# Five bursts of attention scores in place of six, in two of a fused kernel's eight batches

## The chip, the core and the metric

The kernel runs on one core of one Trainium2 chip. The metric is device time in microseconds (us), the whole program from start to end. The core has five engines with a queue each: TensorE (PE in the profile; its weight loads are listed apart as PEld), VectorE (DVE), ScalarE (ACT), GpSimd (POOL) and SyncE (SP). Here POOL and SP do little but issue DMAs. Each engine works its queue in order, and semaphores tell one engine that another is done.

## What is computed

The reference is sigmoid attention followed by a gated feed-forward layer, cut here to what matters:

```python
scores = scale * np.matmul(q, k.transpose(0, 1, 3, 2)) - np.log(S)   # 8 batches, 12 heads, S = 448, head size 64
attn = 1.0 / (1.0 + np.exp(-scores))
x = np.matmul(attn, v)                   # then heads beside each other: 3584 tokens x 768
gate = np.maximum(x @ w_gate, 0.0)       # 768 x 1536
out = (gate * (x @ w_val)) @ w_out       # 1536 x 768
```

## The kernel before, in words

**Units.** The attention of a batch is cut into 21 *units* `(g, c)`: 3 groups `g` of four heads, and 7 chunks `c` of 64 keys. `qk_unit` (line 299 and on) runs a unit: two PSUM banks are taken, `qk` (L239) writes scores for two pairs of heads into them with four matmuls that each use a quarter (64x64) of the PE array and run at the same time, and two sigmoids on ACT (L187), one for each bank, put the result into a tile `PT` in SBUF (11 such tiles, used in turn). When the 7 units of a group are there, `pv` (L257) multiplies them with `v`: 28 quarter-array matmuls into two banks, which DVE copies to `xT` (L184).

**Works.** Between the units PE does the feed-forward layer of batches that are through with attention, in full-array (128x128) matmuls, L389. It comes in *works* taken from a queue by `next_work`. Two kinds matter. `gv_pair`, the gate and value pair (`"w"`, six for each group of two batches), makes two slices of 128 features of gate and value for two batches by a Strassen-like scheme of seven products of six matmuls each, in this order: `u`, `g2`, `u` again, `g1`, `u`, `g2`, `u`. ACT or DVE copies the first `u` (L644), ACT copies `g2` and the second `u` (L624), DVE adds (L628) and makes `hT` (L638). `down_pair` (`"y"`) makes the output from `hT`, also in seven products. Each work prepares on DVE the weight sums of the next (`prepare`).

**Order.** The order on all engines is that in which the Python code issues (`manual_schedule`). The loop over batches `b` = 1 to 7 (L934 and on) cuts the 21 units at `cuts` into bursts. Step `m` issues one burst and then one work, so that ACT can do the burst's sigmoids while PE works. `pv_at` says where in a burst a `pv` is slipped in: at index 2 of burst 0 for the last group of the batch before, of burst 2 for group 0 and of burst 4 for group 1. In batch 4 there are six bursts of 4, 3, 4, 3, 4, 3 units, and the six works are the gate and value pairs of batches 2 and 3. In batch 6 the works are one `down_pair`, with burst 1 in its middle (`inner`), and four gate and value pairs of batches 4 and 5, each behind a burst. So the even bursts have four units and a `pv`, and the odd ones three units.

**Banks.** PSUM has 8 banks. `bank()` hands them out in the order of a queue and puts each at its end; `later` reorders it. A unit or a `pv` takes two neighbours, called a *pair of banks* below. A gate and value pair takes three pairs of banks, for `u`, `g2` and `g1`, and leaves the queue so: the pair of banks it did not use, then `g1`, `g2`, `u`. A burst begins at the head of that queue.

**Transposes and loads.** `dma_transposes(b, g)` makes `qkT` for group `g`: two DVE copies into a tile `rel` (L222) and a transposing DMA from SP (L226). `load` and `load_v` (L111 to L117, POOL) fetch the next batch; `k` and `q` have one buffer, so their loads wait for the last group's `rel` copies. These steps are jobs of a work: they are issued in its middle (`beside`), behind its third product.

The lines that set all this are:

```python
cuts, pv_at = (0, 4, 7, 11, 14, 18, 21), {0: (-1, 2), 2: (0, 2), 4: (1, 2)}
...
for m in range(count):
    jobs, ahead = [], []
    burst(bursts[m])
    if m == (2 if b == 4 else 0) and b > 3:
        jobs.append(lambda: dma_transposes(b, 2))
    ...
    elif 0 <= m - count + 2 and b in (4, 6):
        jobs.append(lambda: dma_transposes(b + 1, m - count + 2))
    ...
    elif m == (2 if b == 4 else 0) and b + 1 < B:   # load(b + 1, ...), load_v(b + 1)
```

Of the kernel before, what the change touches and what calls it, by code (L numbers as in the profile page):

```python
# [18 lines left out]
def kernel(  # L19
# [170 lines left out]
    def qkT_of(b, g):  # L190
        if (b, g) not in qkT_tiles:
            qkT_tiles[(b, g)] = qkTp.tile([P, TW, P], FP16, tag="qkT", name="qkT")
        return qkT_tiles[(b, g)]
# [24 lines left out]
    def dma_transposes(b, g):  # L218
        k16, q16, _ = in_tiles[b]
        rel = relp.tile([P, TW, P], FP16, tag="rel", name="rel")  # L220
        for ti, t16 in enumerate((k16, q16)):
            nc.vector.tensor_copy(  # L222
                rel[:, ti * NCH : (ti + 1) * NCH, :].rearrange("p c (h d) -> p h c d", h=2),
                t16[:, 2 * g : 2 * g + 2, :].rearrange("p h (c d) -> p h c d", c=NCH),
            )
        nc.sync.dma_start_transpose(  # L226
            qkT_of(b, g)[:], rel[:].rearrange("p c x -> p (c x)")
        )
# [70 lines left out]
    def qk_unit(b, g, c):  # L299
        ps = [bank("qk_ps") for _ in range(2)]  # L300
        qk(qkT_tiles[(b, g)], c, 0, NCH, lambda hh: ps[hh][:, 0:S])
        PT = PTp.tile([P, 2, S], FP16, tag="PT", name="PT")
        for hh in range(2):
            sigmoid(PT[:, hh, 0:S], ps[hh][:, 0:S])
        PT_tiles[(b, g, c)] = PT

    def pv_group(b, g):
        pv(b, g, 0, S, [PT_tiles.pop((b, g, c))[:, :, 0:S] for c in range(NCH)])


    def gv(b, q0, qn, f, act_relu):
        gv_out(b, q0, qn, f, act_relu, [gv_product(b, q0, qn, f, i) for i in range(2)])
# [247 lines left out]
    def early_sum_steps(j, f):  # L560
        views = []
        for i in range(3 * j, 3 * j + 3):
            t = early.tile([P, 2, 512], FP16, tag=f"PT{i}", name="S")
            flat = t[:].rearrange("p a y -> p (a y)")[:, 0 : HD * 2 * P]
            views.append(flat.rearrange("p (x y) -> p x y", y=2 * P))
        yield lambda: gate_sums(f, f + 2)
        yield from unit_sum_steps(("s", f), f, views)
# [292 lines left out]
    def pv_finish(b):  # L860
        pv_group(b, NG - 1)
# [7 lines left out]
    def both(b, g):  # L869
        pe_transposes(b, g, 0)  # L870
        pe_transposes(b, g, 1)
# [32 lines left out]
    def prepare():  # L904
        for step in prepare_steps():
            step()

    def next_work(jobs=(), alone=False, amid=None, ahead=()):
        kind, g, i = work.popleft()

        due = pending[:]
        del pending[:]

        def beside():
            for job in due + list(jobs):
                job()

        for job in ahead:
            job()
        if kind == "y":  # L920
            down_pair(g, i, beside, prepare, not work, scaled_act if alone else scaled, amid)
        elif amid:
            raise ValueError(kind)
        elif kind == "w":
            by = (nc.vector.tensor_copy, nc.scalar.copy)
            gv_pair(g, i, lambda: (prepare(), beside()), (by[alone], by[alone or bool(ahead)]))
        elif kind == "s":
            gv_split(g, i, lambda: (prepare(), beside()))
        else:
            gv(g, 0, S, i, True)  # L930
            beside()
            prepare()

    for b in range(1, B):  # L934
        if b == 1:
            cuts, pv_at = (0, 3, 6, 9, 13, 17, 21), {3: (0, 2), 5: (1, 2)}
        else:
            cuts, pv_at = (0, 4, 7, 11, 14, 18, 21), {0: (-1, 2), 2: (0, 2), 4: (1, 2)}
        bursts = list(range(len(cuts) - 1))
        inner = {}  # L940
        if b > 2:
            inner = {2: 3, 3: 5} if b == B - 1 else {0: 1, 1: 3, 2: 5} if b % 2 else {} if b == 4 else {0: 1}
            for n in inner.values():
                bursts.remove(n)
        count = len(bursts)
        hooks = {}
        if b == 1:
            mix = (4, 3, 3, 3, 3, 4)
            hooks = {
                1: [(3, lambda: both(1, 1))],  # L950
                3: [(3, lambda: both(1, 2))],
                4: [(2, lambda: dma_transposes(2, 0)), (0, lambda: dma_transposes(2, 1))],
                5: [(4, late_loads)],
            }
            steps = itertools.chain.from_iterable(early_sum_steps(j, 2 * j) for j in range(4))
            given = ((0, 0, 1, 1, 1), (0, 1, 1, 1), (0, 1, 1, 1), (0, 1, 1, 0), (2, 0, 0, 0), (0, 1, 1, 1, 0))
        else:
            mix = (0,) * count

        def burst(n):  # L960
            for i, (g, c) in enumerate(order[cuts[n] : cuts[n + 1]]):
                if n in pv_at and i == pv_at[n][1]:
                    if n == 0:
                        pv_finish(b - 1)
                        if b == 2:
                            push_group(0)
                        elif b == 6:
                            push_group(2)
                    else:
                        pv_group(b, pv_at[n][0])  # L970
                qk_unit(b, g, c)

        for m in range(count):
            jobs, ahead = [], []
            burst(bursts[m])
            if m == (2 if b == 4 else 0) and b > 3:
                jobs.append(lambda: dma_transposes(b, 2))
            if b == 2 and m == 3:
                jobs += [lambda: dma_transposes(3, 0), lambda: dma_transposes(3, 1)]
            elif b == 3 and m == count - 1:  # L980
                jobs.append(lambda: dma_transposes(4, 1))
                push_group(1)
            elif b == 5 and m == count - 1:
                jobs += [lambda: dma_transposes(6, 0), lambda: dma_transposes(6, 1)]
            elif 0 <= m - count + 2 and b in (4, 6):
                jobs.append(lambda: dma_transposes(b + 1, m - count + 2))
            if b == 1:
                if m == 0:
                    load(2, 0, 1, "kq")
                    load(2, 1, 2, "kq")  # L990
                    load(2, 2, 3, "kq")
            elif m == (2 if b == 4 else 0) and b + 1 < B:
                for g0, g1 in ((0, 1), (1, NG)) if b == 3 else ((0, NG),) if b > 3 else ():
                    jobs.append(lambda g0=g0, g1=g1: load(b + 1, g0, g1, "kq"))
                jobs.append(lambda: load_v(b + 1))
            if b == 2 and m == 0:
                ahead.append(lambda: split_sums(1))
            elif b == 2 and m == 4:
                open_late()
                first_sums = token_sum_steps(0, 0)  # L1000
                ahead += [*first_sums[:2], lambda: weight_sums(0)]
            elif b == 2 and m == 5:
                ahead += [lambda: weight_sums(1), lambda: dma_transposes(3, 2)]
                jobs += first_sums[2:]
            elif b == 3 and m == 0:
                jobs.append(lambda: (weight_sums(2), weight_sums(3)))
            elif b == 3:
                jobs.append(lambda: gate_sums(6 + 2 * m, 8 + 2 * m))
                if m == 1:
                    jobs.append(lambda: keep_odd(0))  # L1010
            if b % 2 and b > 2:
                if m == count - 1:
                    jobs.append(lambda: (batch_sums_t1(b // 2), batch_sums(b // 2, (0, 1))))
            elif b == 4 and m == 0:
                first, *others = batch_sum_steps(1, (1, HD))
                ahead.append(first)
                jobs = others + jobs
            elif b > 3 and m == 0:
                jobs.append(lambda: batch_sums(b // 2 - 1, (1, HD)))
            if mix[m]:  # L1020
                for job in jobs:
                    job()
                ffn_mix(mix[m], hooks.get(m, ()), steps, given[m])
            else:
                next_work(
                    jobs, ahead=ahead,
                    amid=(lambda: burst(inner[m])) if m in inner else None,
                )
            if b == 3 and m == count - 2:
                dma_transposes(4, 0)  # L1030
    pv_finish(B - 1)
    push_group(B // 2 - 1)
    next_work([lambda: batch_sums(B // 2 - 1, (1, HD))])
# [32 lines left out]
```

## Time and profile before

| what | value |
|---|---|
| time, median of 3 runs | 388.31 us (388.07 to 388.63) |
| the profiled execution | 388.3 us |
| its span, first to last instruction | 386.5 us |
| granted TensorE clock, mean | 0.999 of full speed |
| busy share PE, PEld, DVE, ACT, POOL | 99%, 58%, 79%, 59%, 13% |
| batch 4 in the span | 125.6 to 182.6 us |
| batch 6 in the span | 212.8 to 260.7 us |

The span is 1.8 us less than the profiled execution's own time; what lies around it is start and end. In the timeline each row is a run of like instructions: start, length, engine, line, what is written and read, how many, and in brackets how long the engine sat idle before it and what ended that. Rows of PE overlap, because matmuls are pipelined: the distance between the starts of two rows is the time that PE gives to the first, and the length of a row is a little longer.

### The profile page before, as it was taken

What the parts mean: (1) busy time and instruction counts of PE and PEld (TensorE: products, weight loads), DVE (VectorE), ACT (ScalarE), POOL (GpSimd) and SP (SyncE); (2) the same over time, 40 slices, a digit from 0 to 9 for tenths busy, and PEclk for the clock granted to TensorE, in tenths of its full rate; (3) what the DMA queues carried; (4) which work ended last, traced back from release to release, by engine and by line L of the source; (5) the groups of instructions that cost most, each with busy time, mean ns of one, the idle gap of its engine ahead of it and who ended that gap; (6) DMA issues with size and microseconds to landing.
All of it is one profiled execution on the core that took longest, in us unless ns stands there. A gap on an engine that the chain in (4) does not pass through costs nothing.

```text
span 386.5 us, 8978 instructions
## 1 busy us (share of the span) xinstructions
PE 381.1 (99%) x3570; PEld 223.2 (58%) x3570; DVE 304.9 (79%) x611; ACT 227.3 (59%) x480; POOL 49.8 (13%) x73
## 2 busy tenths in 40 slices
PE   8999999999999999999999999999999999999996
PEld 6678776885555545455555554545455555555654
DVE  3455667769868999999868789999978788999653
ACT  5967887567777645455777764545477344333322
POOL 8643306100400003000300300000000000000000
PEclk9999999999999999999999999999999999999999
DMA  9999999999979302952499893222013220000235
GB/s 171 199 199 204 204 193 161 208 208 135 179 168 178 81 2 37 182 95 47 43 229 220 171 233 56 44 54 50 0 28 76 72 75 0 2 0 0 73 92 165
DMA packets 67563, 43.81 MB, mean 113 GB/s; under 512 B 35648, under 2 KB 64192, under 8 KB 67520
## 3 DMA queue, kind: packets, MB, share of 16 engines
q0 software_dynamic: 28960, 23.24, 39.2%
q1 hardware_dynamic: 37792, 19.34, 24.5%
q10 hardware_dynamic: 768, 0.66, 0.6%
q8 instruction: 28, 0.46, 0.5%
q14 instruction: 15, 0.12, 0.1%
HBM read 47.19 MB, written 11.01 MB: 151 GB/s over the span
## 4 chain that ended last, share of the span: by engine, by line
PE 96%; ACT 2%; DMA 1%; DVE 0%; issue 0%
PE u L389 34%; PE g L389 16%; PE y L389 12%; PE qk_ps L239 10%; PE pv_ps L257 8%; PE g_ps L322 5%; PE v_ps L322 5%; PE u L718 2%; PE g L718 2%; ACT PT L187 2%; DMA qkT<-rel 1%; PE warm_ps L175 1%; PE trt L204 1%; DVE ysb L544 0%; DVE zeros L130 0%
## 5 line engine op out<-in xcount | busy, mean ns | idle before, releaser
L187 ACT ACTIVATE PT<-qk_ps 128x448 f16<-128x448 f32 (+3 forms) x318 | 150.9, 584 | 79.2 <-PE qk_ps L239 79.1
L389 PEld LDWEIGHTS <-S 128*128 128x128 f16 x576 | 56.3, 98 | 45.9
L628 DVE TENSOR_TENSOR gsb<-g,gsb 128x448 f32<-128x448 f32 x72 | 42.7, 623 | 7.9 <-PE g L389 7.5
L239 PE MATMUL qk_ps<-qkT 64*64 64x448 f16 (+2 forms) x756 | 47.5, 337 | 0.7 <-DMA qkT<-rel 0.3
L389 PEld LDWEIGHTS <-hT 128*128 128x128 f16 x318 | 29.5, 98 | 24.0 <-issue 6.1
L257 PE MATMUL pv_ps<-PT,v 64*64 64x448 f16 (+2 forms) x756 | 36.6, 329 | 0.0
L468 DVE SCALAR_TENSOR_TENSOR ysb<-y,ysb 128x384 f32<-128x384 f32 x33 | 18.3, 555 | 20.7 <-PE y L389 14.1
L184 DVE TENSOR_SCALAR xT<-pv_ps 128x448 f16<-128x448 f32 (+2 forms) x53 | 27.8, 566 | 8.0 <-PE pv_ps L257 6.9
L389 PEld LDWEIGHTS <-wg 128*128 128x128 f16 x216 | 20.2, 98 | 21.8 <-issue 4.3
L389 PEld LDWEIGHTS <-wv 128*128 128x128 f16 x216 | 21.1, 98 | 19.7
L450 ACT ACTIVATE ysb<-u 128x384 f32<-128x384 f32 x28 | 13.8, 491 | 30.9 <-PE u L389 26.8
L389 PE MATMUL u<-wo,hT 128*128 128x384 f16 x156 | 29.8, 327 | 0.0
L239 PEld LDWEIGHTS <-qkT 64*64 64x64 f16 x756 | 17.6, 106 | 21.0 <-issue 14.1
L111 POOL DMA_DIRECT2D k<-in_k_dram x14 | 10.8, 775 | 141.0 <-DVE rel L222 135.9
L257 PEld LDWEIGHTS <-v 64*64 64x64 f16 x756 | 21.4, 107 | 11.1 <-issue 0.5
L389 PE MATMUL u<-xT,wg 128*128 128x448 f16 x108 | 23.5, 354 | 0.0
L389 PE MATMUL u<-xT,wv 128*128 128x448 f16 x108 | 23.4, 352 | 0.0
L389 PE MATMUL g<-X,S 128*128 128x448 f16 x108 | 23.4, 352 | 0.0
L389 PE MATMUL u<-X,S 128*128 128x448 f16 x108 | 23.4, 352 | 0.0
L389 PE MATMUL g<-xT,S 128*128 128x448 f16 x108 | 23.4, 352 | 0.0
L389 PE MATMUL g<-xT,wg 128*128 128x448 f16 x108 | 23.4, 352 | 0.0
L389 PE MATMUL u<-X,wv 128*128 128x448 f16 x108 | 23.4, 352 | 0.0
(98 smaller groups left out, 563.9 us busy)
## 6 DMA issues: line engine op xcount, KB each, us to landing
out_dram<-ysb SPq DMA_DIRECT2D x53, 192.0 KB, 3.1
v<-in_v_dram POOLq DMA_DIRECT2D x8, 336.0 KB, 15.3
v<-in_v_dram POOLq DMA_DIRECT2D x16, 168.0 KB, 15.1
k<-in_k_dram POOLq DMA_DIRECT2D x4, 672.0 KB, 11.6
q<-in_q_dram POOLq DMA_DIRECT2D x4, 672.0 KB, 14.8
wo<-in_moe_w_out_dram POOLq DMA_DIRECT2D x2, 1152.0 KB, 19.2
k<-in_k_dram POOLq DMA_DIRECT2D x9, 224.0 KB, 11.8
q<-in_q_dram POOLq DMA_DIRECT2D x7, 224.0 KB, 12.3
```

What stands on the lines that cost most here:

```text
L111: nc.gpsimd.dma_start(t16[:, xs, cs], rows_of(src, b)[:, xs, cs])
L175: nc.tensor.matmul(ps[:, 0:n], zeros[:, 0:P], zeros[:, 0:n], start=True, stop=True)
L184: nc.vector.tensor_scalar(out=xT, in0=src, scalar1=XSCALE, scalar2=None, op0=AOP.mult)
L187: nc.scalar.activation(PT_ap, ps_ap, AF.Sigmoid, bias=sig_bias, scale=qk_scale)
L239: nc.tensor.matmul(out_of(hh)[o : o + 64, :], qkT[rows, c, cols], qkT[rows, NCH + c0 : NCH + c1, cols], start=True, stop=True, tile_positi ...
L257: nc.tensor.matmul(ps[hh][64 * r : 64 * r + 64, 0:qn], v16[rows, 2 * g + hh, c * D : (c + 1) * D], pieces[c][rows, hh, :], start=(c == 0), ...
L322: nc.tensor.matmul(ps[:, 0:qn], (wg, wv)[i][:, dc, f * P : (f + 1) * P], xT_tiles[b][:, dc, q0 : q0 + qn], start=(dc == 0), stop=(dc == ND ...
L389: nc.tensor.matmul(ps[:, 0:n], A[:, k_, :], W[:, k_, :], start=(first and k_ == 0), stop=(k_ == kn - 1), skip_group_check=True,)
L450: nc.scalar.activation(o, ps[:, 0:HM], AF.Copy, scale=OUT_SCALE)
L468: nc.vector.scalar_tensor_tensor(out=o, in0=ps[:, 0:HM], scalar=OUT_SCALE, in1=o, op0=AOP.mult, op1=AOP.add)
L628: nc.vector.tensor_tensor(out=gs[u][i][:], in0=ps[u][:, 0:S], in1=gs[u][i][:], op=AOP.add)
L718: nc.tensor.matmul(ps[j // 2][:, j % 2 * SQ : (j % 2 + 1) * SQ], sets[j][i][:, k_, :], W[:, k_, :], start=(first and j % 2 == 0 and k_ == ...
```

## The change

In batches 4 and 6 the cuts become 0, 5, 8, 13, 16, 21: five bursts of 5, 3, 5, 3, 5 units. The places of `pv` stay at index 2 of bursts 0, 2 and 4. `count` falls by one in both batches, from 6 to 5 and from 5 to 4. The last gate and value pair of each batch (slices 10 and 11 of batches 2 and 3; slices 6 and 7 of batches 4 and 5) now follows the pair before it directly; it is called with `alone=True`, which puts both copies of its first product on ACT rather than DVE, and it has no jobs. In batch 4 the transposes of the last group move from step 2 to step 1. The transposes for the next batch stay in the last two steps of the loop, which are now one step earlier.

```diff
-            cuts, pv_at = (0, 4, 7, 11, 14, 18, 21), {0: (-1, 2), 2: (0, 2), 4: (1, 2)}
+            cuts = (0, 5, 8, 13, 16, 21) if b in (4, 6) else (0, 4, 7, 11, 14, 18, 21)
+            pv_at = {0: (-1, 2), 2: (0, 2), 4: (1, 2)}
...
-            if m == (2 if b == 4 else 0) and b > 3:
+            if m == (1 if b == 4 else 0) and b > 3:
                 jobs.append(lambda: dma_transposes(b, 2))
...
             if b == 3 and m == count - 2:
                 dma_transposes(4, 0)
+        if b in (4, 6):
+            next_work((), True)
     pv_finish(B - 1)
```

## The prediction

> **What bounds the kernel now.** First the page's busy shares and the waits of PE, then the timeline of one stretch of batch 6, engine by engine.
>
> ```profile
> PE 381.1 (99%) x3570; PEld 223.2 (58%) x3570; DVE 304.9 (79%) x611; ACT 227.3 (59%) x480; POOL 49.8 (13%) x73
> ...
> PE 96%; ACT 2%; DMA 1%; DVE 0%; issue 0%
> ```
>
> ```profile
> PE warm_ps L175 <- DVE zeros L130: 1.2, 1, 1.2
> PE qk_ps L239 <- DMA qkT<-rel: 0.3, 1, 0.3
> PE qk_ps L239 <- ACT PT L187: 0.3, 1, 0.3
> ```
>
> The chain that ended last is 96% PE, and PE's waits add up to 1.8 us. So a microsecond that PE gains or loses in batches 4 and 6 is one gained or lost at the end. Now PE, ACT and DVE around a burst of three units, the pair behind it, and a burst of four with a `pv`:
>
> ```profile
> 231.76 1.30 PE L389 MATMUL u<-X,wv 128*128 128x448 f16 x6
> 232.98 0.76 PE L239 MATMUL qk_ps<-qkT 64*64 64x448 f16 x12
> 233.68 1.31 PE L389 MATMUL u<-xT,wg 128*128 128x448 f16 x6
> 234.82 1.30 PE L389 MATMUL g<-X,S 128*128 128x448 f16 x6
> ...
> 241.73 0.57 PE L239 MATMUL qk_ps<-qkT 64*64 64x448 f16 x8
> 242.13 1.49 PE L257 MATMUL pv_ps<-PT,v 64*64 64x448 f16 x28
> 243.45 0.55 PE L239 MATMUL qk_ps<-qkT 64*64 64x448 f16 x8
> ```
>
> ```profile
> 242.21 3.60 ACT L187 ACTIVATE PT<-qk_ps 128x448 f16<-128x448 f32 x8 [4.28 <-PE qk_ps L239]
> 245.85 1.10 ACT L624 COPY gsb<-g 128x448 f32<-128x448 f32 x2
> ```
>
> ```profile
> 242.37 1.15 DVE L638 SCALAR_TENSOR_TENSOR hT<-gsb 128x448 f16<-128x448 f32 x2
> 243.66 1.16 DVE L184 TENSOR_SCALAR xT<-pv_ps 128x448 f16<-128x448 f32 x2
> 244.73 1.17 DVE L644 COPY gsb<-u 128x448 f32<-128x448 f32 x2
> ```
>
> Look at the pace of ACT. PE puts out a unit in 0.19 us; ACT needs two sigmoids for it. Eight took 3.60 us, one alone 0.56, so they start (3.60 - 0.60) / 7 = 0.43 us apart, the last at 0.60: 0.85 us for each unit. Within a burst PE outruns ACT by far, and only the four pairs of banks let it.
>
> **What it saves: two bursts' entry and exit.** A full-array product takes 1.135 us (six matmuls, 233.68 to 234.82), 0.189 for each. The next pair's first product starts at 243.94, so from pair to pair (233.68 to 243.94) it is 10.26 us: 42 matmuls x 0.189 = 7.95, four units and seven rounds of `pv` 11 x 0.189 = 2.08, and 0.23 left. For the burst of three (224.94 to 233.68): 8.74 - 7.95 - 0.57 = 0.22. The row starts say where this lies: PE leaves the last product 0.09 late for the burst (231.76 + 1.135 + 0.09 = 232.98) and the burst 0.10 late for the product. A burst costs about 0.23 whatever its size. Two fewer: **-0.46 us**. The units and products themselves keep their number: in the order of the instructions PE has 7142 rows before and after.
>
> Here a rule of the Trainium skill bears on it: TensorEngine Tiling (Array Packing), section Key Properties, says that a change of the tiling mode drains TensorE. The entry and exit rows agree, with 0.09 and 0.10 us. If each were a full drain of about 175 ns, as TensorE: Matmul & The Clock Gate, section Single matmul latency, has it, two bursts less would be an estimated -0.70 and the sum 389.3; the rows decide.
>
> **What it adds: the fifth unit waits for the second's sigmoids.** Follow the bank queue, as the front describes it: L (left over), A (old `g1`), C (old `g2`), B (old `u`). In a burst with `pv` at index 2 the takers are u0 on L, u1 on A, `pv` on C, u2 on B, u3 on L, and now u4 on A. u4 may not write until both sigmoids of u1 are done. From the rows, with S = 241.73 the burst's start: u2 at S + 1.72, u3 + 1.91, u4 would be at S + 2.10. ACT begins at S + 0.48; u1's second sigmoid is its fourth: start S + 0.48 + 3 x 0.43 = S + 1.77, length 0.56, end S + 2.33 (this row alone, by the timeline: 243.50 + 0.56 = 244.06). From ACT's end to PE's start there are 0.05 to 0.06: the early first-slot sigmoids end at 7.94 + 1.93 = 9.87, and the matmul that waits for them starts at 9.93:
>
> ```profile
> 9.93 0.30 PE L239 MATMUL qk_ps<-qkT 64*64 64x256 f16 x4 [0.28 <-ACT PT L187]
> ```
>
> So u4's second matmul starts at S + 2.38, **0.28 late**. PE's queue is in order: the burst's exit and the pair behind it stand behind that matmul, and nothing hides it. ACT cannot be earlier, as it was idle 4.28 us before the burst and starts when the first unit's matmuls are done. u3 on L is free: u0's sigmoids end at S + 1.46.
>
> There are six such bursts: 0, 2, 4 in both batches. In all, u4's bank is last read by u1's sigmoids. Where a copy to `ysb` precedes the sigmoids (bursts 0 of both and 2 of batch 6) ACT still starts at S + 0.49 to 0.50. Sum: 6 x 0.28 = **+1.69 us**. Bounds for one wait: 0, if the release came 0.28 earlier than these rows say; 0.4, if as much is added as PE waited for the one late transpose (PEld idle for 0.70 at 212.79, 0.32 ahead of the other bursts behind a `down_pair`). I take 0.28, since all its terms are rows of this very burst.
>
> **What else moves, and its cover** (each taken as 0):
> - The pair behind a five-unit burst takes C, B, L. C is read by DVE's two `xT` copies: second ends S + 3.09; the second half of the first product, which needs it, starts at S + 2.10 + 0.28 + 0.29 + 0.57 = S + 3.24. Spare 0.1. B's sigmoids (u2) end near S + 3.2, used at S + 3.8; L's (u3) S + 4.1, used at S + 6.1.
> - ACT has two more sigmoids before the `g2` copies: 0.85 later in ACT's queue, 0.47 later on PE, so 0.4 of delay. The second `u` copies follow and must be done when the fifth product begins, at pair + 4.54. They end 0.1 to 0.4 before it.
> - The lone sixth pair takes L, A, C, all read long before; its first copies on ACT start at 0.73 and 1.3 into the pair, and the third product needs them at 2.27. DVE loses 1.17 of work there.
> - Batch 4's `rel` copies for group 2 and, released by them, SP's transpose and POOL's five loads come one pair earlier (about 9.3 us; POOL only sat waiting, 49.88 us, for these copies). The transpose took 11.9 us beside those loads (150.98 to 162.89); issued at 141.6, it lands at 153.5, and unit 14 needs it at 156. Spare 2.5, against 0.7 before. k and q landed 12.2 and 15.4 after the first load's issue: 157.0, used at 160.4. In batch 6 the copies for batch 7 come about 9 us earlier, at 239; their q lands at 234.4. Uncovered, each microsecond late would cost one, once.
> - `PT`: unit 18's tile is unit 7's, read in the first round of the `pv` just before it, S + 0.6; its sigmoid comes at S + 2.2.
>
> **Sum**, on the profiled execution's 388.3 (span 386.5, 1.8 around it; the median of the runs, 388.31, is the same): 388.3 - 0.46 + 1.69 = **389.5 us**, 0.3% slower. About 0.2% (0.78 us) is what a measurement of this kernel can tell from no change.
>
> **Rivals.**
> 1. *The banks come free in time* (0.12). Only the saving stays: 388.3 - 0.46 = 387.8, not slower. Place: u4's second matmul. It decides if ACT's fourth sigmoid releases its bank at S + 2.05 or before, 0.28 sooner than its row ends. For it: bursts of four never wait for ACT. Against: in a burst of four only u3 takes a pair of banks for the second time, and there it has 0.4 of spare.
> 2. *The backlog reaches the pair too* (0.08). The 0.1 of spare at DVE's `xT` copies or ACT's copies is gone, and each of six pairs loses 0.2 to 0.3 more: 389.5 + 6 x 0.25 = 391.0. For it: DVE has no idle row around bursts, its `hT` rows end only 0.14 before the `xT` rows. Against: with `rel` copies in the pair ahead, DVE is as early at the next burst (before 260.73 it reaches `hT` 0.42 ahead of it, just as before 241.73).
> 3. *A late transpose or load* (0.02): the spares above are used up; 390 to 392.
> 4. *The clock falls* (0.02). PE's granted clock is 9 tenths or more in all 40 slices, and 0.999 in the mean, with a gap of 0.38 us in it. If six new gaps took half the clock for one slice (9.7 us), it would cost 4.8: 394.3. The Trainium skill, TensorE: Matmul & The Clock Gate, section A second HAM failure mode: psum-queue depth-cycling, tells of such a case, where short idles from cycling through banks made the clock oscillate; this trace, with its 0.38 us gap at full clock, doesn't bear it out.
>
> The forecast has 0.76. Its own spread: waits of 0.13 to 0.4 each give 388.6 to 390.2. The range goes to 390.7 to take in half of rival 2; left out are rival 1, the other half of 2, and 3 and 4: 0.20. Slower by over 0.2%: rivals 2 to 4 (0.12) and the forecast but for small waits (0.68), 0.80. Within: 0.08 of the forecast and most of rival 1, 0.17. Faster: 0.03.
>
> **What would show it.** In the profile after, batch 4 as a whole (125.6 to 182.6 before, 57.0 us) takes 57.6. From the start of the second `qk_ps` row of a five-unit burst to the pair's first product it is 0.49 + 0.19 + 0.28 = 0.96 us, and PE's waits name ACT's `PT` six times, 0.3 or less each. The lone pair's first product follows 1.13 after the product before it. ACT's rows in those bursts have 10 sigmoids in 4.45 us. I am wrong if those rows are 0.68 apart (no wait), if PE waits for DVE `xT` in the pair, or if a `qkT` transpose is waited for anew.

## The result, and the profile after

The changed kernel takes **389.99 us** (median of 16 runs, 389.16 to 391.15), the kernel before 388.33 (16 runs beside them). The ratio is 1.0045, with a 95% interval of 1.0037 to 1.0053: 1.4 to 2.1 us slower. The prediction said 389.5, which is 1.2 more than before: the sign and most of the size came out, but the loss is larger than forecast. The profiled execution took 389.97 us, its span is 388.1, and the granted clock 0.999 as before.

The busy shares and the chain's shares on the page of the kernel after:

```profile
PE 382.1 (98%) x3570; PEld 224.5 (58%) x3570; DVE 303.2 (78%) x607; ACT 228.8 (59%) x484; POOL 49.8 (13%) x73
...
PE 95%; ACT 2%; DMA 1%; DVE 0%; issue 0%; ACTq 0%
```

PE has the same 3570 matmuls and still is the chain. DVE lost four copies and ACT won four: the first copies of the two lone pairs. The view of PE's waits after (engine, tile and line that waited, what released it, then us in total, times, longest):

```profile
PE warm_ps L175 <- DVE zeros L130: 1.2, 1, 1.2
PE qk_ps L239 <- DMA qkT<-rel: 0.5, 1, 0.5
PE qk_ps L239 <- ACT PT L187: 0.3, 1, 0.3
PE pv_ps L257 <- ACT PT L187: 0.2, 1, 0.2
```

Here a reader could be led astray. Six new waits for ACT's `PT` were forecast, and this view has none of them: the one of 0.3 is the old one (9.47), and that of 0.2 belongs to a `pv` of before 28.7 us, far ahead of any changed instruction. Yet the time is gone. So look at the starts of rows instead. This is the timeline of the second burst of five in batch 4, PE, its weight loads, ACT and DVE (start, length, engine, line, operation, tiles, how many, idle before):

```profile
144.84 0.57 PE L239 MATMUL qk_ps<-qkT 64*64 64x448 f16 x8
...
145.25 1.49 PE L257 MATMUL pv_ps<-PT,v 64*64 64x448 f16 x28
145.33 3.16 ACT L187 ACTIVATE PT<-qk_ps 128x448 f16<-128x448 f32 x7 [4.28 <-PE qk_ps L239]
...
146.38 0.52 PEld L239 LDWEIGHTS <-qkT 64*64 64x64 f16 x10
146.57 1.04 PE L239 MATMUL qk_ps<-qkT 64*64 64x448 f16 x12
146.78 1.16 DVE L184 TENSOR_SCALAR xT<-pv_ps 128x448 f16<-128x448 f32 x2
147.23 0.11 PEld L239 LDWEIGHTS <-qkT 64*64 64x64 f16 x2 [0.33 <-issue]
...
147.54 0.93 PE L389 MATMUL u<-xT,wg 128*128 128x448 f16 x4
```

and this is ACT's fourth sigmoid of that burst alone, from a narrower window of the timeline:

```profile
146.62 0.56 ACT L187 ACTIVATE PT<-qk_ps 128x448 f16<-128x448 f32 x1
```

The 12 matmuls of u2, u3 and u4 start at 146.57, and the pair's first product at 147.54, 0.97 behind. Three units at 0.189 and an exit of 0.10 would be 0.67. Why it is 0.3 more shows in the weight loads: after ten of them PEld stands idle for 0.33, and the last two come at 147.23. By the single starts, u4's first matmul goes at 146.95, 0.19 behind u3, and the other three together at 147.23. ACT's fourth sigmoid, u1's second, ends at 146.62 + 0.56 = 147.18, 0.05 ahead of that, and that is the wait, 0.28 to 0.29 us. PE itself shows no idle row, since its matmuls overlap: u4's first matmul is drawn 0.35 long, to 147.30, past the start of the next at 147.23, and so covers the gap. The Trainium skill says why in Perfetto Trace Analysis, section Tensor Engine Instruction: the end that the profiler gives to a matmul is computed from its size, not observed. The trace agrees: u4's second matmul follows its first by 0.28 to 0.29 us in five bursts and by 0.44 in the sixth, and none of these left an entry in the waits.

From the burst's start to the pair's first product it is now 2.70 us in five of the six bursts, where a burst of four with `pv` takes 2.21. In the kernel before, the burst of four that starts at 241.73 has its pair's first product here:

```profile
243.94 1.31 PE L389 MATMUL u<-xT,wg 128*128 128x448 f16 x6
```

Of these 0.49 us more, 0.19 is the unit's own time, and 0.30 the wait and what comes with it. The sixth, the first of batch 6, takes 213.39 to 216.37 = 2.98:

```profile
212.94 0.49 ACT L450 ACTIVATE ysb<-u 128x384 f32<-128x384 f32 x1 [0.62 <-PE u L389]
...
213.39 0.57 PE L239 MATMUL qk_ps<-qkT 64*64 64x448 f16 x8 [0.49 <-DMA qkT<-rel]
...
214.16 2.72 ACT L187 ACTIVATE PT<-qk_ps 128x448 f16<-128x448 f32 x6 [0.73 <-PE qk_ps L239]
...
216.06 0.11 PEld L239 LDWEIGHTS <-qkT 64*64 64x64 f16 x2 [0.34 <-issue]
...
216.37 0.34 PE L389 MATMUL u<-wo,odd 128*128 128x384 f16 x1
```

There ACT begins 0.77 behind the burst's start, not 0.49. Nothing stands ahead of it: its copy to `ysb` ended at 213.43. The sigmoids are 0.28 later, and so is the end of u4: its last weights come 2.67 behind the burst's start, against 2.39 in the burst at 144.84.

Stage by stage, from burst start to burst start, before against after: batch 4 57.00 and 57.68 us, batch 5 30.18 and 30.36, batch 6 47.93 and 48.90, batch 7 the same within 0.01. The changed kernel's batch 4 begins 0.27 earlier in its profile, ahead of any changed instruction. The 0.18 of batch 5 is its last wait, for the `qkT` transpose ahead of batch 6: 0.38 before, 0.56 after. In the profiles of the experiments below this wait stands anywhere from 0 to 0.82 us and follows none of the edits (0 in e5 and e8, 0.75 in e6, 0.82 in e4), so it is not put down to the change.

### The profile page after: what moved, and what is told of

It is laid out like the page before. It is cut to its first block, busy times and chain, and to the rows that moved or that the text cites. A ratio compares the mean times of both kernels' runs of the same rounds, so it can differ in the third digit from the quotient of the medians.

```text
span 388.1 us, 8982 instructions
## 1 busy us (share of the span) xinstructions
PE 382.1 (98%) x3570; PEld 224.5 (58%) x3570; DVE 303.2 (78%) x607; ACT 228.8 (59%) x484; POOL 49.8 (13%) x73
## 4 chain that ended last, share of the span: by engine, by line
PE 95%; ACT 2%; DMA 1%; DVE 0%; issue 0%; ACTq 0%
PE u L389 34%; PE g L389 16%; PE y L389 12%; PE qk_ps L239 10%; PE pv_ps L257 8%; PE g_ps L322 5%; PE v_ps L322 5%; PE u L718 2%; ACT PT L187 2%; PE g L718 2%; DMA qkT<-rel 1%; PE warm_ps L175 1%; PE trt L204 1%; DVE qkT L211 0%; DVE ysb L544 0%
## 5 line engine op out<-in xcount | busy, mean ns | idle before, releaser
L239 PE MATMUL qk_ps<-qkT 64*64 64x448 f16 (+2 forms) x756 | 48.9, 336 | 1.2 <-DMA qkT<-rel 0.5
L239 PEld LDWEIGHTS <-qkT 64*64 64x64 f16 x756 | 18.9, 105 | 22.8 <-issue 15.4
L644 ACT COPY gsb<-u 128x448 f32<-128x448 f32 x17 | 9.2, 539 | 32.4 <-PE u L389 32.0
```

Source lines behind the costliest of these rows:

```text
L239: nc.tensor.matmul(out_of(hh)[o : o + 64, :], qkT[rows, c, cols], qkT[rows, NCH + c0 : NCH + c1, cols], start=True, stop=True, tile_positi ...
L644: first_copy[u](gs[u][0][:], b[u][:, 0:S])
```

## The experiments

**Theory A**, as predicted: the fifth unit waits for u1's sigmoids, in each burst of five, and dropping a burst saves 0.23. **Theory B**: the time goes where works and jobs moved, in the lone pair or the transposes and loads, and the fifth unit costs little more than its own time.

Medians of each kernel and of the kernel before beside it, the ratio with its 95% interval, and the bursts:

| run | bursts in batches 4 and 6 | us | before | ratio |
|---|---|---|---|---|
| e1 | batch 4: 5, 3, 5, 3, 5; batch 6 as before | 389.05 | 388.10 | 1.0023 (1.0015 to 1.0031) |
| e2 | batch 6: 5, 3, 5, 3, 5; batch 4 as before | 388.89 | 388.10 | 1.0022 (1.0013 to 1.0031) |
| e3 | 5, 2, 4, 3, 4, 3 in both | 389.80 | 388.10 | 1.0043 (1.0031 to 1.0055) |
| e4 | 4, 3, 4, 3, 4 in both, three units left out | 386.58 | 388.10 | 0.9964 (0.9952 to 0.9975) |
| e5 | as after, two units' sigmoids halved | 388.73 | 388.02 | 1.0017 (1.0007 to 1.0027) |
| e6 | as after, half of one unit's sigmoids halved | 389.22 | 388.02 | 1.0030 (1.0019 to 1.0042) |
| e7 | batch 4: 4, 4, 4, 4, 5; batch 6 as before | 388.61 | 388.02 | 1.0020 (1.0010 to 1.0031) |
| e8 | 5, 3, 3, 3, 4, 3 in both | 388.64 | 388.02 | 1.0016 (1.0006 to 1.0025) |
| e9 | as after, batch 4's lone pair copies on DVE | 389.82 | 388.14 | 1.0046 (1.0032 to 1.0060) |

### One batch at a time

e1 changes batch 4 alone, e2 batch 6 alone (there the transposes of batch 4 stay at step 2):

```diff
-            cuts = (0, 5, 8, 13, 16, 21) if b in (4, 6) else (0, 4, 7, 11, 14, 18, 21)
+            cuts = (0, 5, 8, 13, 16, 21) if b == 4 else (0, 4, 7, 11, 14, 18, 21)   # e2: b == 6
...
-        if b in (4, 6):
+        if b == 4:   # e2: b == 6
             next_work((), True)
```

> The change in batch 4 alone. Theory A (banks: in each five-unit burst the fifth unit waits for the second unit's sigmoids, 0.30 us from the unit before to the pair behind as the profile after has it, and a dropped burst saves 0.23): batch 4 takes 57.0 + 3 x 0.30 - 0.23 = 57.7 us, batch 6 its 47.9 as before; time 388.3 + 0.7 = 389.0. Theory B (the fives cost nothing; the lone last pair and the jobs that come a pair earlier cost the time): half of the whole difference, 0.8 to 0.9, but lying in the lone pair or behind it, with fives 0.68 from second score row to the pair's first product. Open besides: whether the wait for the transpose before batch 6 (0.38 before, 0.56 after) grows from batch 4's change (then it is 0.56 here) or by chance.

> The change in batch 6 alone. Theory A: batch 4 stays 57.0; batch 6 takes 47.9 + 3 x 0.30 - 0.23 = 48.6 us if ACT's late start in its first burst after (0.77 instead of 0.49 us behind the burst's start) was chance, 48.9 if it comes with the change; time 389.0 to 389.3. Theory B: 0.8 to 0.9 more than before, in the lone pair or behind it.

Each batch carries its share: +0.6 to +1.2 us for batch 4, +0.5 to +1.2 for batch 6. In both traces each of the three bursts of five takes 2.70 to 2.71 us. Batch 4 in e1 goes from 125.12 to 182.81, 57.69; batch 6 in e2 from 212.56 to 261.18, 48.62 instead of 47.93. So each batch loses 0.69: three waits of 0.305 less one entry and exit, 0.23.

The late start of ACT in batch 6 comes and goes. In e2 it is absent: ACT begins 0.49 behind the burst there. In e1, where that burst has four units, it is there again:

```profile
212.99 0.57 PE L239 MATMUL qk_ps<-qkT 64*64 64x448 f16 x8 [0.31 <-DMA qkT<-rel]
...
213.75 2.73 ACT L187 ACTIVATE PT<-qk_ps 128x448 f16<-128x448 f32 x6 [0.55 <-PE qk_ps L239]
...
215.22 1.14 PE L389 MATMUL u<-wo,odd 128*128 128x384 f16 x6
```

ACT starts 0.76 behind, and yet the burst takes 2.23 us, only 0.02 over the others. A burst of four has spare for a late ACT, one of five has none: in the kernel after, the same lateness cost 0.28.

### A five without a dropped burst, a dropped burst without a five

e3 and e8 keep six bursts and their works and only make the first one five long, taking the unit from the second (e3) or the third (e8); the transposes of batch 4 stay at step 2. e4 drops the last burst and keeps the others as they were; its units 18 to 20 use `PT` tiles of 15 to 17.

```diff
-            cuts = (0, 5, 8, 13, 16, 21) if b in (4, 6) else (0, 4, 7, 11, 14, 18, 21)
+            cuts = (0, 5, 7, 11, 14, 18, 21) if b in (4, 6) else (0, 4, 7, 11, 14, 18, 21)   # e3
+            cuts = (0, 5, 8, 11, 14, 18, 21) if b in (4, 6) else (0, 4, 7, 11, 14, 18, 21)   # e8
+            cuts = (0, 4, 7, 11, 14, 18) if b in (4, 6) else (0, 4, 7, 11, 14, 18, 21)       # e4
...
-        if b in (4, 6):           # out in e3 and e8, kept in e4
-            next_work((), True)
```

> Six bursts as before, of 5, 2, 4, 3, 4, 3 units in batches 4 and 6: one five in each, no burst dropped, no lone pair, no job moved. Theory A: + 2 x 0.30 = 388.9 us, the wait seen in the first burst of both. Theory B: 388.3, no change.

e3 was a poor experiment. Its two fives take 2.70 each, as expected, but the kernel lost 1.7 us (1.2 to 2.1 by the interval), and two fives explain 0.61. Its waits of PE name another cause:

```profile
PE qk_ps L239 <- ACT ysb L450: 0.6, 1, 0.6
```

The burst of two inside batch 6's `down_pair` turns the bank queue by one pair of banks, and the burst behind it (223.80) starts on banks that ACT is still copying to `ysb`; batch 6 loses 0.65 by it. With 0.61 that is 1.26, near the lower end of the interval, so its median cannot tell the theories apart. e8 leaves the burst inside `down_pair` at three units:

> Six bursts of 5, 3, 3, 4, 3, 3... in full: cuts at 0, 5, 8, 11, 14, 18, 21 in batches 4 and 6, so one five and no burst dropped, and the burst inside batch 6's down_pair keeps its three units (with two, in the run with one five before, PE waited 0.65 us for a bank behind it). Theory A: + 2 x 0.30 = 0.61 us, 388.9 where before is 388.3; the waits lie in the first burst of both batches and nowhere else. Theory B: no change.

By its cuts the bursts are 5, 3, 3, 3, 4 and 3 units. It came out at +0.62, 0.2 to 1.0 by the interval, as expected, and batches 4 and 6 of its trace have nothing else: the two fives take 2.706 and 2.705 us, each batch is 0.31 longer than before, and bursts of the old sizes take what they took. A five costs 0.3 with no lone pair and no moved job in sight.

> Five bursts of 4, 3, 4, 3, 4 units and a lone last pair in batches 4 and 6; the scores of the last three units are left out and those of the three before them are used in their place. Theory A: no wait, two bursts and six units of 0.19 us less, 388.3 - 2 x (0.23 + 0.57) = 386.7 us. Theory B: the cost stays, 388.3 - 1.14 + 1.7 = 388.9 us.

e4 met its number as well: 386.58 where 386.7 was expected, or 1.5 less than the kernel before where 1.6 less was. Batch 4 takes 56.20 us, 0.80 less than before: three units at 0.189 are 0.57, and 0.23 is left for the entry and exit. The lone pair's first product stands 1.14 behind the product ahead of it, in PE's timeline of e4:

```profile
172.74 1.30 PE L392 MATMUL u<-X,wv 128*128 128x448 f16 x6
173.88 1.30 PE L392 MATMUL u<-xT,wg 128*128 128x448 f16 x6
```

With e8 and e4 together theory B falls: dropping the burst, with its lone pair and moved jobs, gains what was forecast, and the fives lose without it.

### Is it really the sigmoids that hold the fifth unit?

In e5 the sigmoids of the first two units of each five do half their columns, in e6 only the first sigmoid of the first unit does. The other half of these columns of `PT` is set to zero by POOL:

```diff
-            sigmoid(PT[:, hh, 0:S], ps[hh][:, 0:S])
+            if ns[hh] < S:
+                nc.gpsimd.memset(PT[:, hh, ns[hh] : S], 0.0)
+            sigmoid(PT[:, hh, 0 : ns[hh]], ps[hh][:, 0 : ns[hh]])
...
-                qk_unit(b, g, c)
+                qk_unit(b, g, c, (S // 2, S // 2) if cuts[n + 1] - cuts[n] == 5 and i < 2 else (S, S))    # e5
+                qk_unit(b, g, c, (S // 2, S) if cuts[n + 1] - cuts[n] == 5 and i == 0 else (S, S))        # e6
```

> The changed kernel, but in the five-unit bursts the sigmoids of the first two units take only the first half of the columns (the other half of their tiles is set to zero by GpSimd, so half of these scores is left out). By the rows of two sizes (448 columns 0.43 us apart, 1024 columns 0.90) half a sigmoid takes 0.19 less: ACT is through with the second unit 3 x 0.19 + 0.19 earlier, at burst + 1.6 instead of 2.34, before the fifth unit comes at 2.10. Theory A: no wait in any five, 0.68 us from the second score row to the pair behind; only the two dropped bursts' 0.46 stays: 387.8 us where before is 388.3. Theory B: as the changed kernel, 390.0.

> The same with one sigmoid cut to half, the first of the burst's first unit: ACT is 0.19 us earlier at the second unit's end. Theory A, as a dose: each wait falls from 0.30 to about 0.12 and the time by 6 x 0.19 = 1.1, to 388.8 to 388.9 us. Theory B: 390.0.

Both missed, and alike: in both, the fives take 2.61 us (in e6 but for the one with the late ACT, 2.80). What a five costs over its unit shrank from 0.305 to 0.215 and stuck there, whatever the dose. The medians fit that: with -0.46 for the two bursts, 6 x 0.215 gives +0.83 for e5, which measured 0.3 to 1.0 over the kernel before, and with 0.19 for the late ACT +1.02 for e6, which measured 0.7 to 1.6. The timeline of e5 over the same burst as above shows u4 on time, with its weights loaded in one run, and the pair late all the same:

```profile
145.30 1.10 ACT L187 ACTIVATE PT<-qk_ps 128x224 f16<-128x224 f32 x4 [4.28 <-PE qk_ps L239]
...
146.35 0.49 PEld L239 LDWEIGHTS <-qkT 64*64 64x64 f16 x12
146.54 0.74 PE L239 MATMUL qk_ps<-qkT 64*64 64x448 f16 x12
...
147.43 0.92 PE L391 MATMUL u<-xT,wg 128*128 128x448 f16 x4
```

Row 146.54 is 0.74 long where it was 1.04 in the kernel after, and PEld has no break: u4 no longer waits. What holds the product at 147.43 is DVE's first `xT` copy, alone in a narrow window of e5:

```profile
146.75 0.62 DVE L184 TENSOR_SCALAR xT<-pv_ps 128x448 f16<-128x448 f32 x1
```

It ends at 147.37, and the product starts 0.06 later, on the bank that this copy has read out. So there are two waits, one inside the other: behind the sigmoids' 0.305 stands 0.215 for DVE's copy.

DVE is not late with it through a backlog. In the kernels before and after, in every burst with `pv` of batches 4 and 6, the first `xT` copy starts 1.93 behind the burst's start: with DVE busy until 0.14 before it, as in the burst of 241.73, and with DVE idle ahead of it, as in that of 222.73 (before) and that of 213.39 (after):

```profile
224.66 1.16 DVE L184 TENSOR_SCALAR xT<-pv_ps 128x448 f16<-128x448 f32 x2 [0.71 <-PE pv_ps L257]
```

```profile
215.32 1.16 DVE L184 TENSOR_SCALAR xT<-pv_ps 128x448 f16<-128x448 f32 x2 [0.68 <-PE pv_ps L257]
```

It starts when the `pv` is done, takes 0.62, and the product can start 0.06 later: 1.93 + 0.62 + 0.06 = 2.61, the length of these fives. Theory A holds for the 0.30; that nothing stood behind it was wrong.

### Another cut of 21 units in five bursts

e7 has two bursts of four without a `pv` and a single five (batch 4 alone):

```diff
-            cuts = (0, 5, 8, 13, 16, 21) if b in (4, 6) else (0, 4, 7, 11, 14, 18, 21)
+            cuts = (0, 4, 8, 12, 16, 21) if b == 4 else (0, 4, 7, 11, 14, 18, 21)
...
-        if b in (4, 6):
+        if b == 4:
             next_work((), True)
```

> Batch 4 alone, five bursts of 4, 4, 4, 4, 5 units, no work left out. In the bursts of four without pv (the second and fourth) the fourth unit takes the pair of banks that the pair's last product left, which DVE's two hT instructions read until 0.73 us behind the burst's start; the unit would come at 0.57: theory A gives each a wait of about 0.24 with the staggered exit, the last burst 0.30, and - 0.23 for the dropped burst: batch 4 takes 57.0 + 0.55 = 57.55 us, the time 388.9. Theory B: as in the change in batch 4 alone, since the lone pair and the jobs are the same, 57.7 and 389.0, with no wait in the bursts.

The loss is +0.6 us, 0.4 to 1.2 by the interval; batch 4 takes 57.64, where 57.00 + 0.55 was expected. The first burst of four without `pv`, in PE's timeline of e7:

```profile
136.06 1.31 PE L239 MATMUL qk_ps<-qkT 64*64 64x448 f16 x16
137.29 1.31 PE L389 MATMUL u<-xT,wg 128*128 128x448 f16 x6
```

It takes 1.24 us and the second one 1.10; four units at 0.189 and the usual 0.13 to the product would be 0.88. They lose 0.36 and 0.21, and the last burst, of five, 0.30. What the fourth unit waits for is the pair of banks that DVE still reads for `hT`, in DVE's timeline of e7:

```profile
135.78 1.14 DVE L638 SCALAR_TENSOR_TENSOR hT<-gsb,u 128x448 f16<-128x448 f32 x2
```

These two end at 136.93, and the fourth unit's second matmul starts at 136.98; in the second burst the two times are 156.33 and 156.38. With one burst saved that is +0.64. Both cuts into five bursts that were run thus cost more in waits than the 0.23 they save.

### The late ACT in batch 6

In the five kernels with a late start at batch 6's first burst (after, e1, e5, e6, e7: 0.77 to 0.78 behind the burst) that first sigmoid is record 447 of those that the trace has of ACT, counted from 0 and with its semaphore records. In those with ACT on time it is record 443, and 438 in e4. Record 575, 128 further on, starts late by as much where it is the first after an idle time (after, 281.29: a burst of four, 0.02 lost). Batch 4's lone pair brings the shift of four: its two copies on ACT, each with a semaphore record. So e9 leaves these two copies on DVE:

```diff
-            next_work((), True)
+            next_work((), b == 6)
```

> The changed kernel, with the two first copies of batch 4's lone pair on DVE again instead of ACT, so that ACT's queue has four records fewer (two copies and their waits) ahead of batch 6. In the profiles so far ACT's first sigmoid of batch 6 starts 0.77 us behind its burst instead of 0.49 wherever it is record 447 of ACT's queue (the changed kernel, batch 4 alone, 4-4-4-4-5, short one), and at record 575 in batch 7 (the changed kernel, short both, short one), and never in the kernels in which those records stand inside a run of sigmoids. If the late start belongs to the place in ACT's queue: here the first sigmoid of batch 6 is at 0.49, its five takes 2.70 us instead of 2.98, and the time is 0.28 less than the changed kernel's, 389.7 where before is 388.3. If it is chance, or comes with the fives: 2.98 in some profiles, 390.0 in the mean.

ACT is on time, 0.49 behind, and the burst is as long as the other fives, 212.88 to 215.58, in the timelines of ACT and then of PE of e9:

```profile
213.37 4.47 ACT L187 ACTIVATE PT<-qk_ps 128x448 f16<-128x448 f32 x10
```

```profile
212.88 0.57 PE L239 MATMUL qk_ps<-qkT 64*64 64x448 f16 x8
...
215.58 1.15 PE L389 MATMUL u<-wo,odd 128*128 128x384 f16 x6
```

But the median hardly moved, since batch 4's lone pair now loses what was gained. Its third product, and ahead of it DVE's first copy of the first:

```profile
175.95 1.30 PE L389 MATMUL g<-X,S 128*128 128x448 f16 x6
177.30 1.29 PE L389 MATMUL u<-X,S 128*128 128x448 f16 x6
```

```profile
176.63 0.62 DVE L644 COPY gsb<-u 128x448 f32<-128x448 f32 x1
```

The copy ends at 177.25, since DVE had the `hT` of the pair before to make first, and the product that reuses the bank starts at 177.30, 1.35 behind the one before it and not 1.13. So `alone=True` is worth 0.21 here, and in these traces it costs 0.28 elsewhere by a shift of ACT's queue. The lateness follows the place in the queue in all eleven traces; what makes record 447 late is not settled. The Trainium skill, Runtime: NRT & Kernel Launch, section Instruction fetch mechanics, says that instructions are fetched in blocks of 256 and that this is mostly hidden. The two late places are 128 records apart, and no run here shows a fetch; that it is one was not tried.

## Why the prediction was right

- *Two bursts less, -0.46*: right. e4 has 0.23 for each. The estimate of -0.70, from a full drain at each change, is not borne out by it.
- *The fifth unit's wait, 6 x 0.28 = +1.69*: the mechanism is right, and its times to 0.01 us. u1's second sigmoid starts at S + 1.78 and ends at S + 2.34 (1.77 and 2.33 predicted), and row to product is 0.97 (0.96). As a price it was low: a five costs 0.305 over its unit, 0.28 of it the wait and 0.024 a longer exit (from the last unit's late matmuls to the product 0.306, from the end of other bursts 0.282): 6 x 0.024 = 0.15 not in the sum.
- *ACT still starts at S + 0.49 to 0.50 behind a copy to `ysb`*: failed in one burst of six, the first of batch 6: 0.77, for 0.28 more. Of the two this is the larger miss, and the sum had nothing for it. With both, -0.46 + 6 x 0.305 + 0.28 = +1.65, and the profiles say 0.68 + 0.97 = 1.65 for batches 4 and 6; the measured ratio gives 1.4 to 2.1 us.
- *The cover of what else moves*: held. The lone pair's first product follows 1.13 behind the one before it (173.86 to 174.99), and in no trace does PE wait for the moved transposes or loads. The ten sigmoids take 4.47 us, 4.45 predicted.
- *PE's waits would name ACT's `PT` six times*: wrong. The waits were there, but that view shows no gap that the drawn length of the matmul before it covers; batch 4's 57.68 (57.6 predicted) and the row starts can.
- *Rival 1, banks in time, 387.8*: did not come, and its price was wrong. With the sigmoids out of the way DVE's `xT` would still hold the pair for 0.21, so it would have been 388.3 - 0.46 + 6 x 0.215 = 389.1, slower as well. The working gave this copy a spare of 0.1, but with u4's wait in front of it; without that wait the spare is gone.
- *Rival 2*, a backlog on top of the wait: not seen, and the idle rows ahead of `xT` (224.66 before, 215.32 after) speak against its ground that DVE has none around bursts. The copy that lies beneath the wait follows the end of `pv`.
- *Rivals 3 and 4*: not seen. The clock was 0.998 to 1.0 in every profile, with idle times up to 0.8 us.

## What to carry to other kernels

How long a burst may be is set by how soon its ring of buffers comes round against the pace of the engine that empties them: here a burst less saves 0.23 us, and each burst that is one unit too long loses 0.30. Where a wait is taken away, look for the next one beneath it: its price is the floor, and it is seen only if the spare of every later reader is worked out without the first wait. And a schedule that uses up the spare of each burst makes small hiccups count, as the late ACT did, at 0.02 us in a burst of four and 0.28 in one of five.

## What the runs showed of the hardware

- Here short waits of PE left no idle row and no entry in the waits: 0.28 us in five bursts, and the longer one in the sixth, showed only in the starts of rows and in PEld's idle of 0.33 to 0.34.
- ACT started 0.28 us later than elsewhere at record 447, and again at 575, of its queue, where that record came first after an idle time. In the kernels where another record was the first sigmoid of that burst, it started on time.
- From the end of the ACT or DVE instruction to the start of the PE work that waits for it there were 0.05 to 0.06 us in each of these waits (147.18 to 147.23, 147.37 to 147.43, 177.25 to 177.30, 136.93 to 136.98).
